# Two FFT-mix layers on one core: the last inverse pair evicted by cosine and sine halves, the first row tiles loaded one by one

## The chip, the cores and the metric

The kernel runs on one core of a Trainium2 chip. The metric is the device time of one execution in microseconds (us); the time of a version is the median of its runs. TensorE (PE) multiplies, with its weight loads shown as PEld; VectorE (DVE), ScalarE (ACT) and GpSimd (POOL) do the elementwise work; SyncE (SP) and ScalarE issue the DMAs, GpSimd some of them.

## The reference, cut to what matters

x has 2048 rows of 448 bf16 numbers. Two kinds of layers alternate, each with a layer norm in front and a residual sum behind:

```
def A(x, w_r, w_i):                       # mixing, S = 2048 rows, D = 448
    X = rfft2(x.astype(float32))          # 2048 x 225 complex
    X = X * (w_r + 1j * w_i)              # elementwise filter
    return irfft2(X, s=(2048, 448)).astype(bfloat16)

def B(x, w1, b1, w2, b2):                 # F = 1792
    h = x @ w1 + b1
    r = where(h > 0, h, 0)
    return (r * r) @ w2 + b2

x = x + A(layernorm(x), w_r, w_i)
x = x + B(layernorm(x), w1, b1, w2, b2)
x = x + A(layernorm(x), w_r, w_i)
x = x + B(layernorm(x), w1, b1, w2, b2)
```

## The kernel before, in words

x lies in `xin` as 16 row tiles of 128 rows. The transform is done by matrices of cosines and sines, in stages that pass through PSUM (`ps`, eight banks) and are copied ("evicted") from there to SBUF in bf16 by ScalarE (L706) or VectorE (L707):

- **Row transform** (`first_A`, L866 to L881, called per tile from the loop at L1397). For each row tile: statistics of the rows (VectorE's `BATCH_NORM_STATS2` at L825, or for a few tiles two passes of ScalarE at L847 and L848), the root (L700), the reciprocal (L856), a copy `Fs` of the small matrix `FA` scaled with each row's 1/std (L717 on ScalarE, L718 on VectorE or GpSimd), five matmuls of 256 columns (two with `xin`, two with a raw shifted copy of x that lies in `VT` at this time, one with twice the mean), and one eviction of 512 columns into `XA`.
- **stage_TD** (L953): the column transform for pairs of frequencies, evicted into `arena`. **stage_B** (L976) combines the parts (matrices `G`, `GN`), evicted into `arena` too.
- **stage_W** (L1018): products of the spectrum with the filter, all on VectorE, 28 instructions a transform (`tt`, L735), with the filter's blocks in `Wt`. Its last item, p = 0, uses the block `W08`.
- **stage_Bi** (L1056): first half of the inverse, matmuls with `H`, evicted into `VT`. The axis order of `VT` is (lb, g, t, c, j): lb is the parity of the row, g is 0 for cosine and 1 for sine, t is one of 16 groups, c one of 16 components, j one of 8. Pairs with p > 0 are evicted whole. The last pair, p = 0, has two matmul groups of its own, one for each lb, whose PSUM columns lie as (c, g, t, j); one lb's evictions go to VectorE and the other's to ScalarE (`EV["Bi0"]`), each in two pieces.
- **stage_TI** (L1088), the column inverse: for each t and g, matmuls that read `VT` at all 16 components of that g and t, with the matrix `TI`. **stage_AI** (L1110) is the row inverse with `FI`; then come the residual sum (L1147), the norm and the tiles of the two dense layers with `W1` and `W2`.

The second transform does the same on 16 tiles whose rows come from the first dense layers; there the row transform runs between the last of those.

The program is a list of numbered units (one unit is an instruction or a group of matmuls that share a PSUM tile), and each engine's order is written out by hand: `ORDER` has one list of unit numbers for each engine. Engines wait for one another by semaphores; within an engine nothing overtakes. Fillers (`warm_mm`, L1415, matmuls of a tile of ones) are put in where the planner sees TensorE wait. The DMAs on SP and ScalarE's queue are units as well (`dma`, L658). The loads of x (L765 to L768) come first, then `TD`, `G`, `GN`, the filter's blocks `Wt`, `H`, `TI`, `FI`, the biases, `W1` and `W2`. Two loads wait for the landing of another: the bias rows that complete `W1` wait for the 64 rows of `W1` beside them, and the filter's blocks wait for the two gathers that GpSimd issues (L780).

## Time and profile before

| what | value |
|---|---|
| time, median of 3 runs | 266.68 us (266.57 to 267.13) |
| the profiled execution | 267.61 us, span 265.0 us |
| TensorE busy | 255.3 us (96%), 2127 matmuls |
| VectorE busy | 203.7 us (77%), 653 instructions |
| ScalarE busy | 175.8 us (66%), 380 instructions |
| GpSimd busy | 14.2 us (5%), 32 instructions |
| DMA | 16.33 MB, mean 62 GB/s |
| granted TensorE clock | 1.0 |

The span is the time from the first to the last recorded instruction of one execution; the time of a run has some 2.6 us more around it. A row of the timeline gives the start and the length of a group of like instructions, the engine, the line, the operation, output and inputs by their names in the program, the count, and in brackets how long the engine stood idle before it and what it waited for. Starts are given from the span's start. Instructions of an engine overlap by some hundredths to a tenth of a microsecond, so a group's length is more than the sum of its steps.

### The profile page before, as it was taken

What the parts mean: (1) busy time and instruction counts of PE and PEld (TensorE: products, weight loads), DVE (VectorE), ACT (ScalarE), POOL (GpSimd) and SP (SyncE); (2) the same over time, 40 slices, a digit from 0 to 9 for tenths busy, and PEclk for the clock granted to TensorE, in tenths of its full rate; (3) what the DMA queues carried; (4) which work ended last, traced back from release to release, by engine and by line L of the source; (5) the groups of instructions that cost most, each with busy time, mean ns of one, the idle gap of its engine ahead of it and who ended that gap; (6) DMA issues with size and microseconds to landing.
All of it is one profiled execution on the core that took longest, in us unless ns stands there. A gap on an engine that the chain in (4) does not pass through costs nothing. (4 is left out here: it accounts for less than half of the span.)

```text
span 265.0 us, 5678 instructions
## 1 busy us (share of the span) xinstructions
PE 255.3 (96%) x2127; PEld 160.4 (61%) x2127; DVE 203.7 (77%) x653; ACT 175.8 (66%) x380; POOL 14.2 (5%) x32
## 2 busy tenths in 40 slices
PE   6999989999999999999999998899999999999996
PEld 2786678787544554455567775788654475554454
DVE  3988998999978973779996999899974239832552
ACT  5987898987549448793326988899645886311830
POOL 8840000000000000000000000000000000000000
PEclk9999999999999999999999999999999999999999
DMA  7999700023300223000000000020341000033022
GB/s 224 388 279 342 254 0 2 0 42 71 74 2 0 43 40 66 17 0 2 0 1 2 2 0 2 0 41 5 64 92 37 5 0 2 0 89 97 18 76 82
DMA packets 25531, 16.33 MB, mean 62 GB/s; under 512 B 18174, under 2 KB 24542, under 8 KB 25504
## 3 DMA queue, kind: packets, MB, share of 16 engines
q1 hardware_dynamic: 24768, 14.25, 20.4%
q10 hardware_dynamic: 576, 0.92, 1.0%
q0 software_dynamic: 160, 0.81, 0.7%
q8 instruction: 17, 0.28, 0.4%
q14 instruction: 10, 0.08, 0.1%
HBM read 10.46 MB, written 1.84 MB: 46 GB/s over the span
## 5 line engine op out<-in xcount | busy, mean ns | idle before, releaser
L681 PE MATMUL ps<-yT,W_sb 64*128 64x512 bf16 (+1 forms) x770 | 90.4, 346 | 0.0
L681 PE MATMUL ps<-W_sb,arena 128*128 128x448 bf16 (+3 forms) x476 | 87.1, 342 | 0.0
L681 PEld LDWEIGHTS ps<-yT,W_sb 64*128 64x128 bf16 (+1 forms) x770 | 52.6, 95 | 34.2 <-ACT arena L700 1.3
L735 DVE TENSOR_TENSOR arena<-arena 128x512 bf16<-128x512 bf16 (+1 forms) x140 | 44.8, 366 | 31.0 <-ACT arena L700 30.6
L681 PEld LDWEIGHTS ps<-W_sb,arena 128*128 128x128 bf16 x476 | 45.3, 98 | 38.3 <-DVE arena L735 1.5
L700 ACT ACTIVATE arena<-ps,b1col 128x512 bf16<-128x512 f32 x84 | 52.2, 688 | 24.5 <-PE ps L681 24.4
L706 ACT ACTIVATE arena<-ps 128x448 bf16<-128x448 f32 (+1 forms) x40 | 26.0, 717 | 5.5 <-PE ps L681 5.2
L700 ACT ACTIVATE mv<-mv,epst 128x1 f32<-128x1 f32 (+1 forms) x45 | 12.8, 294 | 14.7 <-DVE mv L826 13.4
L1171 ACT ACTIVATE VT<-x_sb 128x448 bf16<-128x448 bf16 x29 | 16.8, 582 | 5.5 <-DVE x_sb L1147 5.5
L700 ACT ACTIVATE arena<-ps 128x256 bf16<-128x256 f32 x56 | 17.9, 397 | 1.4 <-PE ps L681 1.1
L717 ACT ACTIVATE arena<-x_sb,rstd 128x448 bf16<-128x448 bf16 x13 | 8.8, 673 | 14.9 <-DVE rstd L1216 10.4
L706 ACT ACTIVATE XA<-ps 128x512 bf16<-128x512 f32 (+1 forms) x27 | 14.3, 581 | 4.3 <-PE ps L681 4.3
L681 PE MATMUL ps<-H_sb,arena 128*128 128x256 bf16 x128 | 15.9, 273 | 1.3 <-DVE arena L735 0.9
L681 PE MATMUL ps<-arena,G_sb 128*128 128x448 bf16 (+1 forms) x84 | 16.4, 335 | 0.2 <-ACT arena L706 0.2
L681 PE MATMUL ps<-yT,VT 64*128 64x512 bf16 x42 | 15.8, 376 | 0.0
L706 ACT ACTIVATE VT<-ps 128x1024 bf16<-128x1024 f32 (+2 forms) x20 | 14.1, 786 | 2.2 <-PE ps L681 2.1
L735 DVE TENSOR_TENSOR tmp<-arena,Wt 128x896 bf16<-128x896 bf16 x26 | 15.4, 622 | 0.1
L1293 DVE SCALAR_TENSOR_TENSOR x_sb<-ps,mv,arena 128x448 bf16<-128x448 f32 (+2 forms) x13 | 8.3, 645 | 9.3 <-PE ps L681 9.2
L681 PEld LDWEIGHTS ps<-H_sb,arena 128*128 128x128 bf16 x128 | 11.9, 98 | 4.9 <-DVE arena L735 2.9
L681 PE MATMUL ps<-TD_sb,XA 112*128 112x112 bf16 (+3 forms) x232 | 14.3, 230 | 0.3 <-DVE arena L707 0.3
L706 ACT ACTIVATE tmp<-ps 128x896 bf16<-128x896 f32 (+1 forms) x16 | 12.9, 849 | 1.5 <-PE ps L681 1.5
L681 PEld LDWEIGHTS ps<-TD_sb,XA 112*128 112x128 bf16 (+3 forms) x232 | 12.3, 103 | 2.2 <-DVE arena L707 0.5
(84 smaller groups left out, 298.5 us busy)
## 6 DMA issues: line engine op xcount, KB each, us to landing
out_dram<-x_sb SPq DMA_DIRECT2D x15, 112.0 KB, 1.8
W_sb<-in_B_w_dram SPq DMA_DIRECT2D x1, 1568.0 KB, 12.4
W_sb<-in_B_w_dram SPq DMA_DIRECT2D x1, 1344.0 KB
xin<-in_A_x_dram ACTq DMA_DIRECT2D x4, 224.0 KB, 5.5
xin<-in_A_x_dram SPq DMA_DIRECT2D x4, 224.0 KB, 7.0
H_sb<-c_H SPq DMA_DIRECT2D x1, 896.0 KB, 7.0
G_sb<-c_G SPq DMA_DIRECT2D x1, 672.0 KB, 9.5
Wt<-in_A_w_i_dram SPq DMA_DIRECT2D x1, 393.8 KB, 5.6
```

Of the source, the lines that this page charges most:

```text
L681: return sch.add("pe", lambda e: e.matmul(_res(o), lhsT, rhs, start=start, stop=stop, skip_group_check=skip), [lhsT, rhs], [o], cost=cost, ...
L700: sch.add("act", lambda e: e.activation(o, _res(i), func, **kw), rd, [o], cost=c)
L706: op = sch.add(engs[0], lambda e: e.activation(o, _res(i), ACT.Copy) if h[0].eng == "act" else e.tensor_copy(o, _res(i)), [i], [o], cost=c ...
L717: op = sch.add(engs[0], lambda e: e.activation(o, i, ACT.Copy, scale=s) if h[0].eng == "act" else e.tensor_scalar(o, i, s, 1.0, op0=ALU.mu ...
L735: sch.add(eng, lambda e: e.tensor_tensor(o, _res(a), b, op), [a, b], [o], cost=_free(o) / rate + 69.0)
L1171: op = sch.add("act", lambda e, i=i, o=o, x=x, h=h: e.activation(o, x, ACT.Square, accum_out=sd[:, i, 1:2]) if h[0].eng == "act" else e.sc ...
L1293: small(lambda e: e.scalar_tensor_tensor(out=o, in0=_res(i), scalar=rs[0] if rs else 1.0, in1=xi, op0=ALU.add if t >= 4 and last else ALU. ...
```

## The change

Three things are changed.

1. The loads of x. Before, eight transfers of two row tiles each, alternately on SP and ScalarE's queue, with `FA` behind the first on SP. After, the row tiles 0, 2, 1, 3 come in transfers of one tile (0 and 1 on SP, 2 and 3 on ScalarE's queue), the other twelve in six transfers of two, and `FA` stands behind tile 1 on SP.
2. The evictions of Bi's last pair. Before, each lb's PSUM tile is copied in two pieces by component (c = 0, then c = 1), with both g in each piece: 256 elements for each partition, written in runs of 8. After, it is copied in two pieces by g (cosine, then sine), with both components in each: 256 elements for each partition again, read as two separate stretches of PSUM and written in runs of 16.
3. All five lists of `ORDER` are replaced. There are two units more (two more transfers), so most unit numbers are shifted by 2; beyond that the order differs in many places. Which engine takes which eviction is decided there as well. Among the differences: one of the eight raw copies of x is on ScalarE instead of GpSimd; VectorE evicts three and ScalarE one of the first column tiles' four halves, where it was two and two; the small product on `mv` no longer stands between VectorE's last evictions of the second Bi; an eviction into `XA` stands ahead of VectorE's first casts of the second transform's column tiles; the opening fillers are twelve of 512 columns, one of 256 and one of 128, then the first row tile, then one each of 512, 256 and 128; on SP the loads of `GN`, `FI` and `G` come ahead of `TD`, and the order at the end of the loads is `H`, `W1`, `W2`, the 64 rows of `W1`, the bias rows, b1, and last the imaginary part of `W08`.

The diff, cut to its core (the lists of `ORDER` to their first rows, SP's and GpSimd's nearly whole):

```
--- before.py
+++ after.py
@@ -114,62 +114,62 @@
 ADJ = {}
 ORDER = {
     "pe": """
-54 70 62 104 78 107 86 94 117 120 143 146 130 133 159 156 161 165 162 166 185 171 169 207 181 187 183 189 199 201 211
...
+80 56 72 64 106 109 88 122 119 96 145 148 132 135 161 158 167 163 168 164 187 171 173 183 209 189 191 185 201 203 213
...
     "act": """
-5 7 11 2 9 72 56 66 57 50 58 73 100 88 74 82 103 89 106 90 113 63 93 139 79 87 126 71 108 152 118 147 121 131 134 157
...
+7 4 9 2 11 13 74 75 52 76 58 68 59 55 60 102 90 84 105 91 115 92 87 81 25 65 141 89 128 123 73 154 110 149 120 133 162
...
     "dve": """
-0 64 1 65 48 98 49 96 68 52 59 99 51 97 75 80 60 102 67 81 109 76 111 83 84 101 112 110 135 137 92 115 91 136 138 124
...
+0 50 1 51 66 54 77 53 78 67 98 100 61 70 69 99 101 82 62 104 83 111 113 112 86 114 103 124 93 117 94 125 85 139 137
...
     "pool": """
-12 15 13 16 17 14 18 20 19 22 21 53 69 61 23 77 24 85 25 116 119 26 142 145 129 132 158 155""",
+14 18 15 16 17 19 20 21 22 79 24 71 23 63 28 26 108 118 121 95 27 144 147 131 134 160 157""",
     "sp": """
-3 6 4 8 10 28 30 29 36 32 40 41 39 31 27 34 45 37 33 47 46 38 44 35 314 334 269 352 354 355 372 390 408 426 1005 1026
...
+3 5 6 8 10 12 32 41 36 31 30 38 29 42 40 34 33 35 37 46 49 47 48 43 39 316 336 354 356 357 374 392 410 428 271 1007
...
@@ -762,9 +762,9 @@
         memset(epst[:, 0:1], EPS)
         act(warm[:, 0:1], warm[:, 0:1], ACT.Sqrt)
         sch.table_deps = [sch.last_write[k] for k in _pages(warm[:, 0:1])][:1]
-        for i in range(8):
-            dma("act" if i % 2 else "sp", xin[:, 2 * i:2 * i + 2, :], x_dram[:, 2 * i:2 * i + 2, :])
-            if i == 0:
+        for i, (a, n) in enumerate([(0, 1), (2, 1), (1, 1), (3, 1)] + [(a, 2) for a in range(4, NT, 2)]):
+            dma("act" if i % 2 else "sp", xin[:, a:a + n, :], x_dram[:, a:a + n, :])
+            if i == 2:
                 dma("sp", FA_sb[:], dc["FA"])
@@ -1079,10 +1079,9 @@
                                z[:, c, h, lb:2 * P:2], H_sb[:, c, h, :], h == 0, h == 1)
                     u = None
-                    for c in range(2):
-                        u = evac(VT[:, lb, :, :, c, :],
-                                 q[lb][lambda b, c=c: ps[:, b, c * 256:(c + 1) * 256].rearrange(
-                                     "p (g t j) -> p g t j", g=2, t=16)], EV["Bi0"], u)
+                    for g in range(2):
+                        u = evac(VT[:, lb, g, :, 0:2, :], q[lb][lambda b, g=g: ps[:, b, :].rearrange(
+                            "p (c g t j) -> p g t c j", c=2, g=2, t=16)[:, g]], EV["Bi0"], u)
```

More of the change, by code (lines that the diff above doesn't have):

```diff
@@ L116 @@
     "pe": """
[10 rows of a table removed]
-1354""",
-    "act": """
[12 rows of a table removed]
-1310 1313 1315 1318 1320 1323 1325 1330 1328 1335 1333 1338 1340""",
-    "dve": """
[23 rows of a table removed]
-1339 1341 1346 1255 1343 1119 1349 1352 1355""",
[10 rows of a table added]
+1356""",
+    "act": """
[12 rows of a table added]
+1315 1317 1320 1310 1327 1325 1322 1330 1332 1337 1335 1340 1342""",
+    "dve": """
[23 rows of a table added]
+1338 1103 1336 1341 1343 1348 1307 1345 1351 1354 1357""",
     "pool": """
-12 15 13 16 17 14 18 20 19 22 21 53 69 61 23 77 24 85 25 116 119 26 142 145 129 132 158 155""",
+14 18 15 16 17 19 20 21 22 79 24 71 23 63 28 26 108 118 121 95 27 144 147 131 134 160 157""",
     "sp": """
-3 6 4 8 10 28 30 29 36 32 40 41 39 31 27 34 45 37 33 47 46 38 44 35 314 334 269 352 354 355 372 390 408 426 1005 1026
-1044 1046 1064 1047 1082 1100 1306 1303 1118 1297 1300 1206 1203 1250 1347 1259 1256 1212 1253 1350 1209 1344 1353
-1356""",
+3 5 6 8 10 12 32 41 36 31 30 38 29 42 40 34 33 35 37 46 49 47 48 43 39 316 336 354 356 357 374 392 410 428 271 1007
+1028 1046 1048 1066 1084 1049 1102 1120 1305 1205 1214 1211 1208 1255 1252 1258 1261 1308 1299 1302 1349 1352 1346
+1355 1358""",
 }
```

84 rows, old and new, of the table ORDER are left out of this document.

## The prediction

> **What bounds the kernel now.** I read the page's busy table first, then the chain of waits, the table by stage, and the timelines of the stages in which the table shows slack.
>
> ```profile
> PE 255.3 (96%) x2127; PEld 160.4 (61%) x2127; DVE 203.7 (77%) x653; ACT 175.8 (66%) x380; POOL 14.2 (5%) x32
> ```
>
> TensorE is busy for 255.3 of 265.0 us, so less than 10 us can be won without taking work off it. Where they lie is seen from busy time by stage (columns: stretch, its length, then busy us of PE, PEld, DVE, ACT, POOL with instructions, granted clock, DMA share, GB/s):
>
> ```profile
> 0.00:4.84 4.84, 3.86 (x11) 1.31 (x11) 0.28 (x2) 1.71 (x3) 3.79 (x11) 1.00 0.62 190
> 4.84:8.08 3.24, 1.83 (x7) 0.75 (x8) 3.21 (x17) 3.24 (x13) 3.04 (x7) 1.00 1.00 356
> 8.08:17.05 8.97, 8.80 (x81) 7.61 (x80) 8.36 (x39) 8.50 (x24) 7.36 (x16) 1.00 1.10 351
> 17.05:42.50 25.45, 23.76 (x200) 16.88 (x197) 22.74 (x46) 21.01 (x33) 0.00 (x0) 1.00 0.59 182
> 142.00:148.00 6.00, 5.49 (x105) 4.01 (x104) 3.59 (x16) 4.78 (x12) 0.00 (x0) 1.00 0.01 3
> 148.00:167.20 19.20, 17.36 (x172) 12.50 (x169) 18.66 (x39) 17.15 (x26) 0.00 (x0) 1.00 0.01 2
> 167.20:265.00 97.80, 95.49 (x752) 57.08 (x752) 60.72 (x174) 55.80 (x125) 0.00 (x0) 1.00 0.17 41
> ```
>
> Three places have slack: the start up to the end of the row transform (8.08 us before the first real matmul; PE's 1.83 us in the second row are fillers on a tile of ones), the filter stage of the first transform (25.45 us with 23.76 of PE) and that of the second (19.20 with 17.36). In both filter stages VectorE is the fullest engine beside its own waits. From 167.20 on PE has no waits that count. The chain says the same (start, length, what):
>
> ```profile
> 163.88 1.72 PE ps L681 x14
> 165.62 0.52 DVE VT L707
> 166.22 0.18 DVE mv L735
> 166.40 0.67 DVE VT L707 x2
> 167.16 95.54 PE ps L681 x752
> ```
>
> The last 95.54 us are one dense run of matmuls, released by the two halved evictions of Bi's last pair (each 0.67 / 2, about 0.33 us a step), behind a small product on `mv` (166.22), which holds them up by 0.09: the timeline starts them at 166.31.
>
> ```profile
> 166.31 0.75 DVE L707 CAST VT<-ps 128x256 bf16<-128x256 f32 x2
> ```
>
> So whatever is won ahead of 167.16 is won in the total, one for one; the same holds for the first transform, whose column-inverse matmuls start at 42.26 and from whose stage onward PE is nearly dense.
>
> **The start.** Rows of PE, then of VectorE, ScalarE and SP's queue:
>
> ```profile
> 0.98 3.86 PE L1416 MATMUL ps<-ones 128*128 128x512 bf16 x11 [0.98 <-POOL ones L748]
> 6.08 0.39 PE L1416 MATMUL ps<-ones 128*128 128x512 bf16 x1 [1.25 <-ACT mv L700]
> 6.64 1.61 PE L1416 MATMUL ps<-ones 128*128 128x512 bf16 x6 [0.16 <-DVE mv L826]
> ...
> 4.62 0.63 DVE L825 BATCH_NORM_STATS2 st<-xin 128x6 f32<-128x448 bf16 x1 [3.77 <-DMA xin<-in_A_x_dram]
> 5.38 1.12 DVE L825 BATCH_NORM_STATS2 st<-xin 128x6 f32<-128x448 bf16 x2
> 10.42 1.16 DVE L825 BATCH_NORM_STATS2 st<-xin 128x6 f32<-128x448 bf16 x2 [0.61 <-DMA xin<-in_A_x_dram]
> ...
> 4.62 0.58 ACT L847 ACTIVATE arena<-xin 128x448 bf16<-128x448 bf16 x1 [0.99 <-DMA xin<-in_A_x_dram]
> 14.90 3.06 ACT L706 ACTIVATE XA<-ps 128x512 bf16<-128x512 f32 x6
> ...
> 0.72 0.87 SPq L673 DMA_DIRECT2D xin<-in_A_x_dram  x2
> ```
>
> VectorE and ScalarE both begin at 4.62, when the first two-tile transfers (one on each queue, 448 KB together) are in. The change puts 224 KB ahead of the first statistics. At the 190 to 356 GB/s of the first two stages the missing 224 KB are 1.2 to 0.6 us; the fixed part of a transfer can't be seen apart, and the records cover other transfers too, so I take 0.45 (bounds 0 and 0.8). Each queue has one more issue, of 0.43 us (0.87 / 2), ahead of the later tiles, so that these could come up to 0.4 later.
>
> The new order also sends one tile through statistics, scale and matmuls before it starts on the next, where the old one did the statistics of two to three before the first product. That brings the first real matmul from 8.08 to about 7.0: from data to product it took 8.08 - 4.62 = 3.46, of which the statistics of two further tiles (5.38, 1.12) drop out, which makes 2.34 behind 4.17, so 6.5; other engines' steps in between that VectorE's 1.12 hid make it 7.0 by my estimate. This 1.1 us does not arrive at the end. The stage is as full as its engines: in 8.08 to 17.05 PE is busy 8.80 of 8.97 us, ScalarE 8.50, VectorE 8.36, and the pair of tiles that VectorE waits for at 10.42 (0.61 us) is issued no earlier. ScalarE also takes over one of the eight raw copies of `xin` from GpSimd (by its 128x512 evictions, 3.06 / 6, about 0.5 us). So on ScalarE 0.45 is won and 0.5 is spent, with 0.99 of idle time ahead of it, and the last eviction, at 14.90 + 3.06 = 17.96, moves by something between +0.2 and -0.6. I take -0.2: the first bank is there a microsecond earlier, so evictions can fill ScalarE's and VectorE's gaps earlier, but no engine has less to do. Fewer fillers in the start cost nothing by themselves: they stand in front of real work only where PE would wait.
>
> **From row transform to filter.**
>
> ```profile
> 18.63 1.16 DVE L707 CAST arena<-ps 128x448 bf16<-128x448 f32 x2 [0.94 <-PE ps L681]
> 21.63 0.69 DVE L735 TENSOR_TENSOR tmp<-arena 128x448 bf16<-128x448 bf16 x2 [0.33 <-ACT arena L706]
> ...
> 19.02 0.98 ACT L706 ACTIVATE arena<-ps 128x448 bf16<-128x448 f32 x2 [1.06 <-PE ps L681]
> 21.05 1.35 ACT L706 ACTIVATE arena<-ps 128x448 bf16<-128x448 f32 x2 [1.06 <-PE ps L681]
> ...
> 20.09 0.92 PE L681 MATMUL ps<-arena,G_sb 128*128 128x448 bf16 x4
> ```
>
> Before, two of the first four column tiles' evictions are on each engine, and the first B matmuls start at 20.09, behind ScalarE's second (19.02 + 0.98 = 20.00). In the new order the first B group uses one eviction of ScalarE and one of VectorE: it can go at about 19.02 + 0.49 = 19.51. VectorE's first product at 21.63 waited 0.33 us for ScalarE's eviction of that B group (21.05 + about 0.5), and so follows it: 0.3 to 0.5 earlier here, and with the 0.2 of the start 0.45 to 0.6. Against it: VectorE takes a third cast of about 0.6 in between, which could hold it to 21.5. I take -0.45 for the two together (bounds -0.1 and -0.8).
>
> This gain is kept, since from 21.63 VectorE runs on without a wait to the end of the stage, with the same 28 products (order inside changes only):
>
> ```profile
> 40.72 1.44 DVE L707 CAST VT<-ps 128x512 bf16<-128x512 f32 x3
> ...
> 41.84 0.66 ACT L706 ACTIVATE VT<-ps 128x256 bf16<-128x256 f32 x2 [0.22 <-PE ps L681]
> ...
> 42.26 1.81 PE L681 MATMUL ps<-TI_sb,VT 112*128 112x224 bf16 x22 [0.46 <-ACT VT L706]
> ```
>
> **The halved evictions.** Both halves stay at 256 elements for each partition, so I keep 0.33 us a step on ScalarE (0.66 / 2) and about 0.37 on VectorE. Before, every column-inverse matmul of the next stage needs both the cosine and the sine rows of a component; now the cosine matmuls need only the first half of each engine. At 42.26 PE starts behind ScalarE's first half (41.84 + 0.33 = 42.17) and stumbles behind the second (42.50): 22 matmuls span 1.81 where the eviction's end at 42.50 and dense issue would give 0.2 less. Four matmuls of 224 columns, about 0.08 each, cover the second half: -0.2. In the second transform both halves are waited for at 167.16, so one step of 0.33 goes, less what the second half then delays after two matmuls (0.16): -0.15 to -0.33, and ScalarE is the next to be late, with its own end at 163.06 + 4.12 = 167.18:
>
> ```profile
> 161.34 1.02 ACT L706 ACTIVATE VT<-ps 128x1024 bf16<-128x1024 f32 x1 [1.17 <-PE ps L681]
> 162.26 0.91 ACT L706 ACTIVATE arena<-ps 128x896 bf16<-128x896 f32 x1
> 163.06 4.12 ACT L706 ACTIVATE VT<-ps 128x1024 bf16<-128x1024 f32 x7
> ```
>
> The reading is strided now and the writing contiguous over 16 elements instead of 8. A row for such an operand isn't there: every 1024- and 512-wide eviction of the same buffers already writes 16-element runs at the usual rate (0.52 for 512 columns), and the bounds are -0.05 and +0.2 for each half; I take 0. The `mv` product leaves the chain (-0.09). Behind ScalarE's last wait a 1024-wide eviction stands in place of the 896-wide one (a step of 0.92, 161.34 to 162.26, for one of 0.80: +0.12), which matters only as far as ScalarE is the later of the two. One cast of `XA` goes ahead of the second transform's casts, so its products begin 0 to 0.2 earlier (0.1). Sum for the second transform: -0.2 - 0.09 - 0.1 + 0.12, about -0.25 (bounds +0.1 and -0.6).
>
> **The sum.** -0.45 for start and first B group, -0.2 for the first transform's halves, -0.25 for the second: -0.9. The profiled execution took 267.61 (span 265.0 and 2.6 around it), which becomes 266.7; it is 0.93 above the median of the runs, 266.68, and the same difference there gives 265.8. A difference under 0.2%, 0.53 us, can't be told from none.
>
> **Rivals.**
> *The gain of the start is absorbed.* If the row transform ends when it did, because ScalarE pays the raw copy in full and the later tiles' data arrive as before (0.61 of waiting at 10.42), VectorE's third cast then also holds the products to 21.5: only some 0.1 and the 0.45 of the halves stay, 266.2, and with strided reads at +0.1 each 266.4. For it: the busy shares of the stage. Against it: 0.99 and 0.33 us of visible waiting that the new order answers. Chance 0.22.
>
> *TensorE falls back to its slow pace.* The first row of PE has 11 fillers in 3.86 us, (3.86 - 0.39) / 10 = 0.35 apart, the later one 6 in 1.61, (1.61 - 0.39) / 5 = 0.24 apart: the same instruction has two paces, at a granted clock of 1.00 in both, and the pause of 1.25 between them did not bring the slow one back. The new order stops its opening fillers at about 5.0 and then waits for the first tile, some 2 us. If the slow pace came back there, warming up again would cost 10 x 0.11 = 1.1 us on PE's part of the row transform, which is what its earlier start wins: the 0.2 of the start go and up to 0.2 are added, 266.0 to 266.2, and 266.6 with a second relapse between the first two tiles. The Trainium skill ("TensorE: Matmul & The Clock Gate", What's actually happening) says that the clock halves after an idle window of about 3.4 us that runs freely; by that rule neither pause is long enough alone, though one with little work before and after might be, and the pace of the first row, 0.35 on the mean, lies between the 0.24 and its double, while the granted-clock column shows no change. Chance 0.08.
>
> *A filter block arrives late: slower.* In the new order of SP's queue the first filter's last two-tile block (the imaginary part) is the last load of all, behind the bias rows, which wait for a landing.
>
> ```profile
> 20.13 0.26 SPq L673 DMA_DIRECT2D W_sb<-in_B_b_dram  x1
> ...
> 21.70 2.47 SPq L673 DMA_DIRECT2D H_sb<-c_H  x1
> ...
> out_dram<-x_sb SPq DMA_DIRECT2D x15, 112.0 KB, 1.8
> ...
> H_sb<-c_H SPq DMA_DIRECT2D x1, 256.0 KB, 11.6
> Wt<-in_A_w_i_dram SPq DMA_DIRECT2D x1, 112.5 KB, 5.4
> ...
> 39.04 1.16 DVE L735 TENSOR_TENSOR tmp<-arena,Wt 128x896 bf16<-128x896 bf16 x2
> ```
>
> Before, the last load was H's 256 KB, issued at 21.7 and landed 11.6 later, at 33.3. In the new order W1's last 64 rows stand behind H's 1.15 MB and the 2.9 MB of W1 and W2 (sizes from the page's table of issues). At 351 GB/s these 4.1 MB take 11.5 us, which from about 14 on is 25.5; if they take as long as all loads did, 33.3. With W1's rows at 33.3 the bias rows, b1 and the block are issued by 34.4 (0.26 and twice 0.43), and the block lands 1.8 us later (as the output's transfers of its size) or 5.4 later (as the block did before): 36.2 to 39.8, or 40.3 if the rows too are half a microsecond behind. It is needed where products with `Wt` start at 39.04, 38.6 by then. At 40.3 everything behind stands for 1.7 us: 267.5. It decides from a landing at 39.5 on, where the 0.9 is gone. Against it: by then the DMA has emptied, and of the pauses that SP makes before, the one for W1's rows (up to 20.13) no longer stands ahead of W1 and W2. Chance 0.09.
>
> *The change is not what it seems.* That the first transfers' sizes decide nothing, because 128 rows of 896 bytes take as long as of 1792, is the bound 0 above. The Trainium skill ("DMA: Bandwidth & Descriptors", Bandwidth) wants transfers of 1 MiB for three quarters of the peak, and gives 0.95 us for 64 KB against 6.15 for 1 MB: that speaks against splitting for the rate, yet by it 112 KB would still land before 224. No row here times a transfer of one tile.
>
> **Chances.** The forecast 0.52 (265.3 to 266.3), absorbed 0.22, slow pace 0.08, late block 0.09; 0.09 for what the reordered row-by-row stages after 42.3 may do unseen, most of it slower. Faster by over 0.2% (under 266.15) takes 0.47 of the forecast, a third of the second and third, and 0.03: 0.59. Slower (over 267.2): most of the late block, most of the unseen, 0.02 of each other rival: 0.16. The rest, 0.25, is the same. The range 265.0 to 267.3 takes in the bounds of the terms and most of the late block's price.
>
> **What would show it.** Right: first statistics near 4.2, first real matmul near 7.0, last row-transform eviction near 17.75, first product at 21.2, column-inverse matmuls at 41.6 to 41.8 and dense, the dense run of the second transform near 166.2. Wrong: fillers or row matmuls at 0.35 apart after 5 us; VectorE idle on `Wt` after 36; a half over 0.45 us; a first product still at 21.6; or new PE waits behind 43 us.

## The result, and the profile after: slower

| | before | after |
|---|---|---|
| median of 12 runs each (range), us | 266.67 (266.51 to 267.29) | 267.98 (266.65 to 269.36) |
| ratio to before, 95% interval | | 1.0046 (1.0033 to 1.0059) |
| profiled execution: its own time, span | 267.61, 265.0 | 267.68, 265.4 |

The forecast was 265.8, in 265.0 to 267.3, with 0.16 on slower. In four of the twelve runs the mean granted clock was 0.994, and those took 268.37 to 269.36; the other eight took 266.65 to 268.19, with a median of 267.69. By the medians, about 1.0 us of the 1.3 is there without those four runs, and 0.3 comes from them.

Up to 172 us the profile after looks like a success. The page's first part, and then the engines' timelines, each at the places that the prediction named:

```profile
PE 256.2 (97%) x2122; PEld 167.0 (63%) x2122; DVE 203.5 (77%) x655; ACT 175.0 (66%) x379; POOL 13.6 (5%) x31
```

```profile
3.28 0.63 DVE L825 BATCH_NORM_STATS2 st<-xin 128x6 f32<-128x448 bf16 x1 [2.43 <-DMA xin<-in_A_x_dram]
...
20.86 0.83 DVE L735 TENSOR_TENSOR tmp<-arena 128x448 bf16<-128x448 bf16 x2 [0.41 <-ACT arena L706]
```

```profile
14.40 3.04 ACT L706 ACTIVATE XA<-ps 128x512 bf16<-128x512 f32 x6
...
160.17 5.84 ACT L706 ACTIVATE VT<-ps 128x1024 bf16<-128x1024 f32 x9
```

```profile
6.75 0.27 PE L681 MATMUL ps<-Fs,xin 128*128 128x256 bf16 x1
...
41.18 1.86 PE L681 MATMUL ps<-TI_sb,VT 112*128 112x224 bf16 x22
...
165.52 1.40 PE L681 MATMUL ps<-TI_sb,VT 112*128 112x224 bf16 x14 [0.20 <-DVE VT L707]
```

The first statistics start at 3.28, the first row matmul at 6.75, the row transform's last eviction ends at 14.40 + 3.04 = 17.44, the first product starts at 20.86, and PE takes up the column inverse at 41.18 without a wait and the second transform's dense run at 165.52. Each is earlier than the prediction asked for (4.2, 7.0, 17.75, 21.2, 41.6 to 41.8, 166.2).

Then PE's timeline behind the second transform shows a wait that the profile of before has nowhere:

```profile
177.94 1.04 PE L681 MATMUL ps<-yT,W_sb 128*128 128x256 bf16 x8
179.81 6.29 PE L681 MATMUL ps<-yT,W_sb 128*128 128x256 bf16 x56 [0.84 <-DMA yT<-x_sb]
186.23 0.54 PE L681 MATMUL ps<-tmp,FI_sb 128*128 128x224 bf16 x4
```

Here is the same place of before. Its matmuls with `yT` run on through 179.81, in a row of 44:

```profile
179.43 0.55 PE L681 MATMUL ps<-tmp,FI_sb 128*128 128x224 bf16 x4
179.81 4.97 PE L681 MATMUL ps<-yT,W_sb 128*128 128x256 bf16 x44
```

The chain that ended last goes, in after, through the DMA transpose that makes `yT`, and so names the transfer: 4.66 us, from its issue on SP at 175.11.

```profile
175.11 4.66 DMA yT<-x_sb
179.76 0.05 issue
179.81 1.06 PE ps L681 x8
```

The view of the tile `yT` gives shortest, median and longest time from issue to landing of its transposes, first of before and then of after. Only after has one at 4.7:

```profile
DMA to landing us min/median/max: 3.0/3.1/3.2
```

```profile
DMA to landing us min/median/max: 3.0/3.1/4.7
```

To see what each stretch gained, the start of each matmul in after was subtracted from that of the same matmul in before. This lead is positive where the run is ahead. "Before again" (below) keeps within 0.03 us of before at every mark up to 257 us, so leads of a tenth mean something. The first column is before's own time.

| mark, before's time | after | after again | 256 fillers | 128 fillers | old halves | some 256 | pairs | pairs + 256 | two singles + 256 |
|---|---|---|---|---|---|---|---|---|---|
| first column transform 17.25 | .49 | -.27 | .33 | -1.11 | .22 | -.59 | .12 | .26 | -.95 |
| first B 20.09 | .84 | .07 | .66 | -.76 | .57 | -.26 | .45 | .59 | -.62 |
| last pair's Bi 40.72 | .70 | -.08 | .50 | -.91 | .42 | -.40 | .30 | .45 | -.76 |
| column inverse 44.69 | 1.02 | .24 | .82 | -.59 | .42 | -.08 | .62 | .77 | -.44 |
| second transform 142.01 | .95 | .17 | .75 | -.66 | .34 | -.15 | .55 | .70 | -.51 |
| its last Bi 166.22 | 1.18 | .40 | .97 | -.44 | .57 | .07 | .78 | .93 | -.28 |
| its inverse 172.15 | 1.44 | .66 | 1.24 | -.18 | .56 | .34 | 1.04 | 1.19 | -.01 |
| next stage 186.75 | .14 | -.56 | .95 | -.46 | -.11 | -.47 | .76 | .26 | -.30 |
| end 259.84 | .09 | -.61 | .91 | -.50 | -.16 | -.51 | .71 | .22 | -.34 |

| mark | halves alone | one filler more | singles alone | singles, a filler less | small packets | singles + 256 |
|---|---|---|---|---|---|---|
| 17.25 | -.16 | .29 | -1.06 | -2.14 | -.09 | -.51 |
| 40.72 | -.16 | .29 | -.86 | -1.77 | -.08 | -.31 |
| 44.69 | .16 | .29 | -.86 | -1.76 | -.07 | -.31 |
| 166.22 | .15 | .28 | -.87 | -1.78 | -.07 | -.30 |
| 172.15 | .42 | .28 | -.87 | -1.78 | -.08 | -.30 |
| 186.75 | .42 | .28 | -.87 | -1.78 | -.07 | -.30 |
| 198.20 | .43 | -.70 | -1.80 | -2.72 | -1.04 | -1.25 |
| 259.84 | .43 | -.70 | -1.80 | -2.71 | -1.04 | -1.89 |

After is 1.44 us ahead at 172 and 0.14 at 187. Behind the last matmuls, on SP, it loses another half microsecond: its last VectorE instruction starts 0.09 earlier than before's, and the span is 0.4 longer. SP's timeline shows the output's transfers there, those of after first and then those of before:

```profile
258.61 5.21 SPq L673 DMA_DIRECT2D out_dram<-x_sb  x8
```

```profile
260.75 2.68 SPq L673 DMA_DIRECT2D out_dram<-x_sb  x5
```

One of after's eight issues, at 258.99, lasted 1.88 us; the others here last 0.33 to 0.46. This half microsecond belongs to the execution and not to the kernel: among all 17 traces only this one and that of `aft_xb` (0.6) lose more than 0.1 at the end, and `after_again`, the same kernel, loses 0.05 there.

### The profile page after: what moved, and what is told of

It is laid out like the page before. It is cut to its first block, busy times and chain, and to the rows that moved or that the text cites. A ratio compares the mean times of both kernels' runs of the same rounds, so it can differ in the third digit from the quotient of the medians.

```text
span 265.4 us, 5660 instructions
## 1 busy us (share of the span) xinstructions
PE 256.2 (97%) x2122; PEld 167.0 (63%) x2122; DVE 203.5 (77%) x655; ACT 175.0 (66%) x379; POOL 13.6 (5%) x31
## 3 DMA queue, kind: packets, MB, share of 16 engines
HBM read 10.46 MB, written 1.84 MB: 46 GB/s over the span
## 5 line engine op out<-in xcount | busy, mean ns | idle before, releaser
L681 PEld LDWEIGHTS ps<-yT,W_sb 64*128 64x128 bf16 (+1 forms) x770 | 59.2, 95 | 27.6 <-DMA yT<-x_sb 1.1
L706 ACT ACTIVATE arena<-ps 128x448 bf16<-128x448 f32 (+1 forms) x38 | 25.0, 735 | 5.6 <-PE ps L681 5.4
```

The lines of the kernel that those rows point to most:

```text
L681: return sch.add("pe", lambda e: e.matmul(_res(o), lhsT, rhs, start=start, stop=stop, skip_group_check=skip), [lhsT, rhs], [o], cost=cost, ...
L706: op = sch.add(engs[0], lambda e: e.activation(o, _res(i), ACT.Copy) if h[0].eng == "act" else e.tensor_copy(o, _res(i)), [i], [o], cost=c ...
```

## The experiments

All results in one place; the ratio is to before, run on the same chip beside each, and can differ by 0.001 from the quotient of the medians.

| what it is | median us (range, runs) | before | ratio (95%) |
|---|---|---|---|
| `after_again`: after, again | 267.53 (266.20 to 268.37, 9) | 266.67 | 1.0022 (1.0007 to 1.0038) |
| `aft_f256`: after, opening fillers of 256 | 267.03 (266.21 to 267.46, 12) | 266.67 | 1.0009 (0.9999 to 1.0020) |
| `aft_f128`: after, opening fillers of 128 | 267.32 (266.43 to 267.74, 8) | 266.67 | 1.0016 (1.0004 to 1.0029) |
| `aft_c`: after, old halves | 267.89 (267.36 to 268.29, 5) | 266.67 | 1.0046 (1.0033 to 1.0059) |
| `before_again`: before, again | 266.72 (266.57 to 267.24, 8) | 266.71 | 1.0001 (0.9989 to 1.0012) |
| `bef_g`: before, new halves alone | 266.29 (265.97 to 266.85, 12) | 266.71 | 0.9981 (0.9972 to 0.9990) |
| `bef_x`: before, new loads alone | 268.75 (268.34 to 268.98, 6) | 266.71 | 1.0072 (1.0059 to 1.0086) |
| `aft_xb`: after, old loads (pairs) | 266.56 (265.94 to 267.54, 12) | 266.71 | 0.9998 (0.9985 to 1.0012) |
| `bef_p`: before, same loads in packets of 896 bytes | 268.12 (267.98 to 268.50, 5) | 266.61 | 1.0055 (1.0041 to 1.0068) |
| `bef_x_f256`: before, new loads, fillers of 256 | 269.52 (268.99 to 270.31, 4) | 266.61 | 1.0116 (1.0097 to 1.0135) |
| `aft_xb_f256`: after, pairs, fillers of 256 | 266.08 (265.82 to 266.93, 8) | 266.61 | 0.9980 (0.9969 to 0.9992) |
| `aft_x1_f256`: after, two single tiles, fillers of 256 | 266.98 (265.83 to 267.73, 12) | 266.61 | 1.0006 (0.9993 to 1.0019) |
| `bef_1f`: before, one opening filler more | 267.73 (267.57 to 267.82, 5) | 266.74 | 1.0038 (1.0025 to 1.0051) |
| `bef_x_18`: before, new loads, one filler less | 268.73 (268.12 to 269.98, 6) | 266.74 | 1.0079 (1.0058 to 1.0099) |
| `aft_f4`: after, only the first fillers of 256 | 267.39 (266.73 to 269.48, 12) | 266.74 | 1.0030 (1.0012 to 1.0048) |

### Does the trace repeat?

`after_again` and `before_again` are the two kernels unchanged.

> The changed kernel once more, unaltered, for a second trace and more times. Its first trace is 1.44 us ahead of the kernel before at the last pair of the second Bi and loses this behind 178 us: 0.84 us in a wait of the matmuls on the DMA transpose issued at 175.11, which landed after 4.66 us instead of 3.1, while the trace shows a 16 KB instruction fetch in the middle of it. Theory A (collision): the collision belongs to the place of the fetch in TensorE's instruction stream, so it is there again: landing over 4 us, median 267.5 to 268.3. Theory B (clock): four of the twelve runs have a granted clock of 0.994 and are the slowest; the loss is the slow clock of some runs, so this trace, if its clock is 1.0, shows a landing of 3.1 to 3.3 us and a span of about 264.3, and the runs at 1.0 are as fast as before or faster.

> The kernel before once more, for a second trace: how far its own start and its DMA transposes vary. Both theories expect the time of before (266.5 to 267.3); the transpose behind the second transform lands 3.1 to 3.2 us after its issue, since the instruction fetch near 175.5 ends before its packets start; the first real matmul lies at 8.08 within 0.3 us.

Before repeats. After does not: its second trace is 0.76 us less ahead by 17.25 and stays so, and then falls by 1.22 at the same transpose. What differs is where the loads land. The last pair of row tiles on SP, tiles 12 and 13, lands at 10.72 in the first trace of after and at 11.49 in the second; in before it lands at 10.39 and 10.42.

### The opening fillers: where a fetch falls

```
-            n = next((n for n in (512, 256, 128) if ...
+            n = next((n for n in ((256, 128) if free["pe"] < 5500.0 else (512, 256, 128)) if ...
```

So in `aft_f256` (23 opening fillers for 14; the same warming time in smaller pieces). In `aft_f128` it is `(128,)` below 5500, and in `aft_f4` `(256, 128)` below 2800 (17 fillers).

> The changed kernel with its opening fillers cut into 20 of 256 columns, 2 of 512 and 1 of 256 (23 instead of 14, about the same time): every later instruction of TensorE stands 9 matmuls (18 instructions) later in the stream, so every fetch comes about 9 matmuls earlier against the work, some 1 us among matmuls of 256 columns. Theory A: the fetch near 176.4 moves to about 175.4, ahead of the transpose's packets (176.4 to 178); landing back at 3.1 to 3.4, no wait of 0.8 us, 0.7 to 1 us faster than the changed kernel. Theory B: no change, 267.7 to 268.3, and again some runs at 0.994.

> As the run with fillers of 256 columns, with 38 of 128 columns and 3 of 512 (41 instead of 14): fetches come 27 matmuls earlier against the work, some 3 us near the transpose. Theory A: fetch near 173.4, transpose undisturbed, 0.7 to 1 us faster than the changed kernel unless a fetch then meets another transpose. Theory B: no change against the changed kernel.

> The changed kernel with its first fillers cut into 7 of 256 columns (17 opening fillers instead of 14, the same time). The fetch near 176.4 lay 1.26, 1.22 and 1.24 us behind the issue of the transpose at 14 fillers, and 1.16 us ahead of it at 23. If the fetch moves with the number of instructions ahead of it alone, it is 0.3 to 0.4 us earlier and still inside: landing over 4 us, 267.5 to 268. If it is clear of the transpose, the landing is 3.1 and the kernel 0.7 to 1.0 us faster than the changed one: 266.6 to 267.0.

The fillers compute nothing that is used, but they are instructions. Queue q8 moves 17 packets of 16 KB in after; PE's two columns of the page hold 2122 + 2122 = 4244 instructions, and 4244 / 17 = 250 for each packet: it is TensorE's program arriving. (The Trainium skill, "Runtime: NRT & Kernel Launch", Instruction fetch mechanics, has instructions fetched in blocks of 16 KiB, 256 each, over a DMA queue of the engine's own; this trace agrees.) The DMA view of after over the 4.69 us of the late transpose, in 40 slices, shows such a packet beside it:

```profile
GB/s 70 0 70 0 0 0 0 0 0 0 231 212 207 205 199 138 37 2 0 0 0 0 0 2 9 9 9 9 11 9 11 199 290 297 275 16 0 0 0 0
...
q1 hardware_dynamic: 1056, 0.26, 71.1%
q8 instruction: 1, 0.02, 2.1%
...
yT<-x_sb SPq DMA_TRANSPOSE x1, 4.7
```

The same transpose in `aft_f256`, over 4.7 us:

```profile
GB/s 70 0 0 0 70 0 0 0 0 0 98 224 218 216 207 220 220 198 211 196 177 46 0 0 0 0 0 0 0 0 0 0 0 0 0 0 0 0 0 0
...
q1 hardware_dynamic: 1056, 0.26, 29.1%
...
yT<-x_sb SPq DMA_TRANSPOSE x1, 3.1
```

Both move the same 1056 packets. With no q8 packet they pass in one stretch and the transpose lands after 3.1 us. With one (it starts 1.26 us behind the issue) the transpose moves half of its bytes, nearly stops for some 1.6 us, and moves the rest; its packets' time is 71.1% of the window for 29.1%. With the transpose on time PE has no wait at 179.81, and the lead falls by 0.29 there instead of 1.30.

The fillers' own size tells nothing more. The fetch had been expected about 1 us away and moved 2.4 (from 1.26 behind the issue to 1.16 ahead of it); in `aft_f4`, with three fillers more, it stayed at 1.26, the landing was 4.2, and the lead fell by 0.81. In `aft_f128` the transpose was on time, and that run lost 1.11 at the start instead. The median of `aft_f256` is 0.95 us under after's and 0.50 under that of `after_again`, which ran beside it; this cannot be split cleanly between the transpose and the runs' different starts. It is still not under before's.

### One more instruction, and nothing else

```
         sch.schedule()
+        d = sch.ops["pe"][1]
+        sch.ops["pe"].insert(1, _Op("pe", d.fn, False, d.cost, 195.0))
         sch.assign_tickets()
```

`bef_1f` is before with one idle opening filler more.

> The kernel before with one filler of 512 columns more among the 18 opening ones, nothing else. Collision theory: as in the run with strided pairs (19 fillers too), the fetch that lies 3.54 us behind the issue of the transpose near 186 comes some 0.9 us earlier, 2.6 to 2.7 behind it, the transpose lands after 4.0 to 4.8 us instead of 3.04, TensorE waits 0.9 us behind it, and one idle matmul costs 0.9 to 1.5 us: 267.6 to 268.1. Rival (the loads did it in the other two): 266.5 to 266.8, landing 3.1.

This settled it: 0.99 us slower, ratio 1.0038 (1.0025 to 1.0051). The lead is +0.28 until the stage at 186 and -0.70 behind it. The fetch comes 2.68 us behind the issue of the transpose there, where in before it comes 3.54 behind. The DMA view over that transpose (4.9 us in 40 slices of 0.12 us) and the times from issue to landing:

```profile
GB/s 0 0 0 0 0 0 0 0 0 10 159 222 228 217 213 192 205 207 201 186 86 15 134 0 0 0 0 0 0 0 0 0 0 0 0 0 0 0 0 0
...
q1 hardware_dynamic: 1056, 0.26, 28.2%
q8 instruction: 1, 0.02, 1.1%
...
yT<-arena SPq DMA_TRANSPOSE x1, 4.7
```

```profile
DMA to landing us min/median/max: 3.0/3.1/4.7
```

The picture differs from after's: here the transpose's bytes have passed by slice 21, 2.6 us behind the issue, the q8 packet follows in slice 22, and what comes late is the landing, 4.7 us behind the issue. The fetch need not cut into the bytes to delay the transpose.

On PE's timeline before's dense run of 42 is broken in two by a wait, which is put down to VectorE's `arena`; that itself follows ScalarE's work on the late `yT`. First before, then `bef_1f`:

```profile
189.78 8.11 PE L681 MATMUL ps<-W_sb,arena 128*128 128x448 bf16 x42
```

```profile
189.50 3.38 PE L681 MATMUL ps<-W_sb,arena 128*128 128x448 bf16 x17
193.69 4.90 PE L681 MATMUL ps<-W_sb,arena 128*128 128x448 bf16 x25 [0.81 <-DVE arena L735]
```

The view of waits, before and then `bef_1f`, has one wait of ScalarE on a transpose more, of 2.4 us:

```profile
ACT arena L717 <- DMA yT<-arena: 4.4, 2, 2.6
```

```profile
ACT arena L717 <- DMA yT<-arena: 6.8, 3, 2.6
```

### The halves and the old halves

`bef_g` is before with the new loop over `g`; `aft_c` is after with the old loop over components, its order unchanged.

```
-                    for c in range(2):
-                        u = evac(VT[:, lb, :, :, c, :], ...
+                    for g in range(2):
+                        u = evac(VT[:, lb, g, :, 0:2, :], ...
```

> The kernel before with the halves by cosine and sine alone (same lists, same loads, same fillers). The first traces of after and of the run with the old halves differ by 0.38 us ahead of the first column inverse and by 0.26 ahead of the second. If the halves are a gain by themselves: lead 0.2 to 0.35 us behind the first and 0.15 to 0.3 more behind the second, total 0.4 to 0.6 us faster than before (266.1 to 266.3). If a later wait (collision of fetch and transpose, whose places shift against each other only by what PE gains) takes it: within 0.2 us of before.

> The changed kernel with Bi's last pair evicted by component again, all else as changed. If the halves by cosine and sine give what was forecast (0.2 us in the first transform, 0.2 in the second), the column inverse starts the same but stumbles: its lead shrinks by 0.2 and then 0.4 us, and the total is 0.4 us slower than the changed kernel, unless a later wait absorbs it. If strided reading costs as much as it saves, no difference. TensorE's instruction count is the same, so under theory A the fetch meets the transpose much as before it.

Alone the halves bring 0.42 us (266.29 for 266.71; the interval, 0.9972 to 0.9990, leaves one out). The leads put it where the prediction did: from -0.16 to +0.16 at the first column inverse and from 0.15 to 0.42 at the second, so 0.32 and 0.27. In `aft_c` the same two steps are 0.00 and -0.01, where after has 0.32 and 0.26. Its median does not show them: 267.89 is not the expected 0.4 above after's, and in its trace the transpose landed after 4.03 us, which cost less than after's 4.66. ScalarE's two halves take as long as before (42.00 here, 41.84 in before, 0.66 in both), and PE starts its inverse with no wait:

```profile
42.00 0.66 ACT L706 ACTIVATE VT<-ps 128x256 bf16<-128x256 f32 x2 [0.22 <-PE ps L681]
```

```profile
42.04 1.86 PE L681 MATMUL ps<-TI_sb,VT 112*128 112x224 bf16 x22
...
166.64 1.31 PE L681 MATMUL ps<-TI_sb,VT 112*128 112x224 bf16 x14 [0.30 <-DVE VT L707]
```

### The loads

```
-        for i in range(8):
-            dma("act" if i % 2 else "sp", xin[:, 2 * i:2 * i + 2, :], ...
+        for i, (a, n) in enumerate([(0, 1), (2, 1), (1, 1), (3, 1)] + [(a, 2) for a in range(4, NT, 2)]):
+            dma("act" if i % 2 else "sp", xin[:, a:a + n, :], ...
```

`bef_x` is before with this alone; its units in `ORDER` are renumbered, with the two added transfers, and otherwise as in before, and 19 opening fillers stand for 18. `aft_xb` is after with the old loop and its order renumbered back. `bef_p` keeps before's eight issues and their sizes, but the first two take row tiles 0 and 2, and 1 and 3, so that each row of 1792 bytes becomes two of 896 (`slice(i, 4, 2)`); it too has 19 fillers.

> The kernel before with the loads of one tile alone, its order of work unchanged (unit numbers shifted; the planner puts in one opening filler more). First statistics at 3.2 to 3.4 instead of 4.6. If data were what the start waited for: row transform ends up to 0.5 us earlier, 266.2. If the order of work and the full engines set it (the forecast's rival): within 0.3 us of before. If the third transfer on ScalarE's queue (tiles 6 and 7), which landed between 5.86 and 7.45 in five traces with these loads, sets it: slower in some runs, a wider spread than before's 264.5 to 265.2 of span.

> The changed kernel with before's eight transfers of two tiles, its order of work and halves kept (unit numbers shifted back; the fillers of the opening become 16 of 512 columns, so their number changes by none against 14 and 3, and fetches stay in place). The collision theory expects the wait on the transpose (0.8 us and more) again. On the start: if the new loads are what makes it vary, the row transform's end is as steady as before's and the spread of the runs shrinks under 0.8 us; if the new order of work makes it vary (it starts tiles 6 and 7 early), the spread stays.

> The kernel before with its eight transfers of two tiles, the first two taking tiles 0 and 2, and 1 and 3, so that their packets are of 896 bytes as with single tiles, with no issue added and the same bytes. With single tiles and before's order the last pair of tiles landed at 11.45 instead of 10.39, and the row transform ended 1.06 us later. If the small packets are what costs: last pair lands 0.7 to 1.1 later here too, total 0.7 to 1.1 us slower than before (plus 0.9 if the stream's 19 opening fillers again put a fetch into the transpose near 187). If the added issue of 0.43 us on each queue costs: last pair within 0.2 of 10.39, and total within 0.3 us of before (or 0.9 slower by that collision alone).

In `bef_x` the start is 1.06 us behind. The last pair on SP lands at 11.45 for 10.39, also 1.06, and VectorE waits for it:

```profile
11.48 1.16 DVE L825 BATCH_NORM_STATS2 st<-xin 128x6 f32<-128x448 bf16 x2 [1.03 <-DMA xin<-in_A_x_dram]
```

(Before waits 0.61 for the same pair, at 10.42.) None of the three expectations had this. In `bef_p` it lands at 10.49 and the start is 0.09 behind: the shorter packets cost next to nothing. By elimination the loss comes from the two added transfers, with one more issue of 0.43 us on each queue and a later place for every pair behind them, and from the place of `FA`, which now goes ahead of tiles 4 and 5. How it splits is not shown: the issue alone explains 0.4, while the same loads put the last pair 1.06 later in `bef_x` and 0.52 later in `bef_x_f256`. Up to 5 us the DMA had moved 964 KB in before, 842 in after and 762 in `bef_x`. In before's order the lead at 17.25 is 10.39 less that landing, to 0.02, in six traces (`before_again`, `bef_g`, `bef_1f`, `bef_x`, `bef_p`, `bef_x_f256`). In after's order with single tiles it is 11.24 less the landing, to 0.03, in five of seven; in `aft_f4` and `aft_x1_f256` another pair was waited for. So the new order bears this pair 0.85 us later than the old, and the new loads deliver it 0.3 to 1.9 later.

Both `bef_x` and `bef_p` fall by 0.93 and 0.97 more near 190, where `bef_1f` does, with a landing of 4.7 us: their fillers moved the same fetch. That is about half of what `bef_x` loses in its trace, and nearly all that `bef_p` loses in its.

In `aft_xb` the collision was expected again and did not come. With as many fillers as after, its fetch starts 1.14 us ahead of the transpose's issue, where after has it 1.26 behind; the landing took 3.05 us, and the lead fell by 0.28 alone. Its runs range over 1.6 us, so the pairs of tiles do not by themselves make the new order steady; whether collisions that come in some runs only make the rest of the spread is not shown.

### Both together

`bef_x_f256` and `aft_xb_f256` have fillers of 256 besides. `aft_x1_f256` is after with row tiles 2 and 3 alone as single transfers, both on ScalarE's queue. `bef_x_18` is `bef_x` with one filler deleted.

```
+        for i, (e, a, n) in enumerate([("sp", 0, 2), ("act", 2, 1), ("act", 3, 1)] +
+                                      [("act" if a % 4 else "sp", a, 2) for a in range(4, NT, 2)]):
...
```

```
         sch.schedule()
+        del sch.ops["pe"][1]
```

> The kernel before with single tiles and its opening fillers cut into 20 of 256 columns and 8 of 512 (28 instead of 19). The run with 19 was 2.0 us slower than before: 0.87 to 1.06 by the start, 0.93 behind the transpose issued at 186.7, which landed after 4.69 us beside an instruction fetch. Collision theory: with the fetch moved by 9 matmuls or more, that transpose lands after 3.1 us again and the kernel is 0.8 to 1.0 us faster than with 19 fillers: 267.7 to 268.0. Otherwise 268.5 to 268.9 again.

> The changed kernel with before's transfers of two tiles and the opening fillers cut into 256 columns: both losses of the changed kernel taken away, its order of work and halves kept. With whole fillers its trace was 1.48 us ahead of before at 178 us, lost 0.43 and 0.29 to places of the new order, and 0.6 at the end where an issue of an output transfer took 2.0 us beside a fetch at 258.6. If losses are the late pair of tiles and the collisions: 0.6 to 0.9 us faster than before, 265.8 to 266.1, and a spread under 0.8 us. If the spread of the changed kernel comes from its order itself: 266.5 as with whole fillers.

> The changed kernel with single tiles on ScalarE's queue only (tiles 2 and 3), tiles 0 and 1 in one transfer on SP, and the opening fillers cut into 256 columns. Half the small packets: by the deficit of 0.34 to 0.56 us of transfer with all four, the last pair should land 0.2 to 0.5 later than in before (10.6 to 10.9), and the row transform ends by the rule seen in the traces of the new order, 11.24 less the landing, 0.3 to 0.6 us ahead of before: 265.8 to 266.2, not better than the run with pairs alone.

> The kernel before with the loads of one tile, and its 18 opening fillers as before. Collision theory: the landing near 186 is 3.1 us again and only the start's loss stays (the last pair of tiles lands 0.5 to 1.1 us later, the row transform ends as much later): 267.1 to 267.7 instead of 268.75. Rival: 268.5 to 269 again.

`aft_xb_f256` is the fastest kernel here, 266.08, ratio 0.9980 (0.9969 to 0.9992), although its profiled execution still had a landing of 4.3 us and fell from 1.19 to 0.26; its runs range over 1.1 us. `bef_g` gains as much with one edit.

The other three came out against their expectations. Nine more fillers left `bef_x_f256`'s fetch where it was (2.65 us behind the issue), and the fall at 190 stayed. It lost another 0.64 behind a second late transpose: issued at 204.25, with a fetch 1.14 us behind it, this one landed after 4.18 us, at 208.43, and PE's next matmuls with `yT` started at 208.53. One filler less did not clear `bef_x_18`. And two single transfers on one queue moved the bottleneck: in `aft_x1_f256` tiles 14 and 15 land at 10.46, GpSimd's copy of them waits 1.27 us, and a piece of `Fs` that PE needs is queued behind that copy. GpSimd's and PE's timelines (the first puts the wait down to PE, whose matmul was long done; the landing is what ends with it):

```profile
10.52 1.06 POOL L707 COPY VT<-xin 128x448 bf16<-128x448 bf16 x2 [1.27 <-PE ps L681]
```

```profile
12.09 0.28 PE L681 MATMUL ps<-Fs,xin 128*128 128x256 bf16 x1 [1.52 <-POOL Fs L718]
```

`bef_x_18` was worth its run for another reason. Its trace caught a run with a mean clock of 0.994. Its busy times by window (PE, PEld, DVE, ACT, POOL, then the granted clock):

```profile
4.18:7.59 3.41, 1.47 (x5) 0.29 (x3) 1.68 (x5) 2.36 (x9) 2.60 (x5) 1.00 0.93 286
7.59:11.00 3.41, 3.40 (x11) 1.55 (x12) 2.88 (x21) 1.90 (x8) 3.41 (x8) 0.50 1.04 409
11.00:14.40 3.40, 3.40 (x33) 3.03 (x32) 2.32 (x9) 3.01 (x10) 1.69 (x4) 1.00 1.07 360
```

For 3.41 us, from 7.59, TensorE ran at half speed, behind a window in which it had been busy for only 1.47 of 3.41 us. The start was 2.14 behind instead of 1.06.

## Why the prediction was wrong, point by point

The first column of numbers is what the sum had, the second is the step of the lead in the first trace of after.

| step | forecast | after's trace | shown by |
|---|---|---|---|
| start of the row transform | +0.2 | +0.49; -0.27 when run again | loads' landings, `bef_x` |
| first B group | +0.25 | +0.35 (0.34 again) | every kernel in after's order |
| B to Bi, "the gain is kept" | 0 | -0.14 | the same |
| halves, first transform | +0.2 | +0.32 | `bef_g`, `aft_c` |
| from there to the second transform | 0 | -0.07 | every kernel in after's order |
| second transform, order and `mv` | +0.05 | +0.23 | every kernel in after's order |
| halves, second transform | +0.2 | +0.26 | `bef_g`, `aft_c` |
| 172 to 187 | 0 | -1.30 | `bef_1f`, `aft_f256` |
| 187 to the end of the span | 0 | -0.5; -0.1 when run again | this execution alone |

**Right: the halves.** The mechanism, the place and the sign held, and the strided reading did cost nothing (0.66 for two halves, as before). The term was undersized, 0.4 for 0.6. It was the part of the change that pays alone.

**Right in sign, with one term off: the order.** Products began earlier as argued (20.86). The sum to 172 was 1.44 in the first trace and 0.66 in the second, where 0.9 was forecast; the first was lucky in its start. That VectorE's 28 products would hold the gain was wrong by 0.14.

**Wrong, and the step that failed: "whatever is won ahead of 167.16 is won in the total".** The prediction read before's list of PE's waits, found none that counted behind 167, and took their absence for a property of the stage. It was a property of where two independent streams happened to fall. A transpose that lands in 3.1 us gives `yT` just in time, and a fetch that starts in the wrong 2 us behind the issue can make it 4 to 4.8. By the traces the new order lost 0.29 in this stage even with the transpose on time (0.28 or 0.29 in `aft_f256`, `aft_f128`, `aft_x1_f256` and `aft_xb`), where PE waits for VectorE ahead of the matmuls at 186.23. The rest goes with the landing: 4.0 us (`aft_c`) costs 0.38 beyond that, 4.2 (`aft_f4`) 0.52, 4.3 (`aft_xb_f256`) 0.64, 4.7 (after) 1.01. That is the landing's excess over 3.1 less about 0.55 of slack each time. The prediction's own list of what would prove it wrong ended with "new PE waits behind 43 us"; one came, but the list gave it no place, price or cause, and all unseen mishaps together had 0.09.

**Mis-sized: the start.** The prediction gave the first data 0.45 of gain and let the later tiles "come up to 0.4 later". The first statistics came 1.3 earlier, 3.28 for 4.62, and that decided nothing, since the last pair decides and came 0.33 later in one trace and 1.10 in the other. The rival in which the start's gain is absorbed (266.2) is close to what the second trace has up to 172, a lead of 0.66. The Trainium skill ("DMA: Bandwidth & Descriptors", Bandwidth), whose preference for large transfers the prediction set aside as a matter of rate, had the sign right; `bef_p` shows that here the cost was not that of smaller packets, which leaves the added transfers.

**The slow pace of TensorE**, given 0.08, did occur, in some runs only: 4 of 12 of after, where the median of those four is 1.2 above the median of the others. Over all runs it was 8 of 74 in kernels with four single tiles (none of the nine of `after_again`), and none in any kernel that loads pairs, before's own runs included. Only the trace of `bef_x_18` shows the half clock itself; for after's four runs it is inferred from the mean clock. The prediction leaned on the Trainium skill's window of 3.4 us ("TensorE: Matmul & The Clock Gate", What's actually happening) and judged neither pause long enough. The steps of 3.41 us agree with that page. The trace adds that the window needs no full pause: there 43% of activity was not enough, while in `aft_f128` a step of 3.41 us with TensorE busy for 1.66 (49%), from 6.10 to 9.51, was not followed by a slow one. The prediction's 0.35 between the first fillers of before is a mean of two paces: the starts in the trace are 0.43 us apart up to 3.52, and 0.21 from 3.81 on. The step comes at another time in each trace; in after the fillers stay 0.43 apart up to 6.07, so that the prediction's sign of the slow pace, fillers 0.35 apart after 5 us, is there without a relapse.

**The late filter block** did not occur; VectorE's products with `Wt` have no wait in after. **That the change is not what it seems** holds in part: packet size decides nothing, as it said, but issues do.

**Open.** That fetch and transpose fall together is shown, and so is the price. What sets the fetch's place is not: one filler moved it by 0.86 us, nine moved it by 2.4 in one kernel and by nothing in another, and equal numbers of fillers left it in two places (after and `aft_xb`). Nor is it shown why the last pair's landing differs by 0.8 us between two executions of after. The traces account for part of the times only: after's traced execution stands 1.0 above before's median while its span is 0.4 longer than that of before's trace. Of the 0.6 between, 0.3 is before's trace, whose span of 265.0 is longer than the median of 264.7 in the 23 runs of before beside `after_again`. The other 0.3 lies outside the span, 2.0 us in most runs of before (the 2.6 is that of its traced execution alone) and 2.2 to 2.3 in after's; its cause was not followed.

## What to carry to other kernels

When an edit changes how many instructions TensorE has ahead of a transfer with little slack, even by one idle matmul, look at the landings of that transfer in the new trace before crediting or blaming the edit: here that was worth 1 us, more than any term of the change. "No wait in the trace of before" says that slack was enough at that alignment; ask how much there is, and what a landing a microsecond and a half later would cost. For a chain of loads, sum to the landing of the load that is waited for last, counting the issues queued ahead of it, not to the first data.

## What the runs showed of the hardware

**A DMA transpose beside an instruction fetch.** Over 17 traces there are 238 transposes of `yT`, all alike. 223 land after 3.02 to 3.44 us. The other 15 take 4.01 to 4.83, and in each of these a 16 KB packet of q8 starts 0.86 to 2.81 us behind the transpose's issue. The converse: of the nine with a fetch 0.86 to 1.26 behind, all are late; of the twelve with one at 2.54 to 2.97, six are. The Trainium skill ("Runtime: NRT & Kernel Launch", Instruction fetch mechanics) calls the cost of crossing such a block "mostly hidden". That holds here for TensorE itself, whose every wait of over 0.15 us behind 45 us follows another engine or a transfer, and not for the transpose beside it. A late landing costs only what exceeds the slack: four of the 15 cost nothing, among them the longest, 4.83 us in `aft_f128`.

**Issues beside a fetch.** SP's issues of output transfers take 0.33 to 0.59 us in 270 cases and 0.9 to 2.2 in 19. All 19 long ones overlap a q8 packet, and so do 11 of the short ones; after's at 258.99 met one at 259.01 that lasted 1.49 us. No experiment of its own changed this.

**The clock.** In the one trace that caught it, half speed lasted one step of 3.41 us and followed a step in which TensorE was busy for 43%; a step with 49%, in `aft_f128`, was not followed by it.
